# A decayed recurrence and two MoE layers on one core: the first 46 slots issued from a table of single operations, with six shared PSUM banks

## The chip, the core and the metric

The kernel runs on one core of a Trainium2 chip. The core has a matrix engine (TensorE, PE in the rows, with its weight loads as PEld), VectorE (DVE), ScalarE (ACT), GpSimd (POOL) and SyncE (SP), whose queue issues the transfers here. Each engine executes its own queue in order, and the engines wait for each other by semaphores. Times are device microseconds of one execution; less is better.

## The reference

What is computed, cut to what matters: a recurrence over 768 steps (2 batches, 8 heads, state 48 x 48), its output as 1536 tokens of 384 columns, a first two-layer MoE on them, and a second MoE with eight experts, whose weights P come from gates that are normalised by rows and columns eight times.

```python
for t in range(S):                       # r, k, v, w: [2, 8, 768, 48]
    cur = np.einsum('bhd,bhe->bhde', u[None] * kt, vt)
    y[:, :, t] = np.einsum('bhd,bhde->bhe', rt, state + cur)
    state = wt[:, :, :, None] * state + np.einsum('bhd,bhe->bhde', kt, vt)
x = y.transpose(0, 2, 1, 3).reshape(1536, 384)
h = x @ w_in                             # float64 weights, 384 x 2048
x = np.maximum(0.01 * h, h) @ w_out      # 2048 x 384
for e in range(8):                       # second MoE
    out += P[:, e:e + 1] * (np.maximum(x @ w1[e], 0.0) @ w2[e])
```

## The kernel before

**Recurrence.** The 1536 tokens are twelve tiles of 128 steps (`NBLK`), the two batches in turn. A tile is worked in chunk form by `att_steps` (L318): w, k and r are transposed on TensorE (four transposes each); VectorE makes the decays by two scans along time (L351, L355) and weighs K and R with them (L358, L361); TensorE forms scores (L382) and transposes K (L394); VectorE masks the scores (L400, two operations); TensorE forms the outputs from them and from the decayed state (L415, L426) and the next state (L435); VectorE adds (L446, L459); TensorE transposes y (L469), and ScalarE and VectorE write it as a rounded high part and a low part (L262, L263), which are the input of the first MoE.

**Weights of the first MoE.** They come as float64. A piece of 768 columns is loaded as words (L225) and put together by integer operations: four on VectorE (L231, L232, L235, L242), three on ScalarE, two on GpSimd (L247, L253). There are 16 such pieces, two staging buffers and two temporaries.

**Units of the first MoE.** A unit is one quarter of the hidden layer for 256 tokens; there are 24, in the list `order`. Each has two p1 slots (18 matmuls of 256 columns each, L497, into a bank `hb`, then relu parts: ScalarE L1003, VectorE L1004, ScalarE L1011, GpSimd L1012) and three p2 slots (12 matmuls each, L512, into `ybm`, then a sum into `x2f` on ScalarE L1023 or VectorE L1025). The p2 slots of a unit stand behind the p1 slots of the next one.

**What sets the order.** `slots` lists all p1 and p2 slots. The steps of the tiles and the pieces are attached to slots by number, in `ATT_AT`, `STEP_AT` and `PIECE_AT` (L778 to L780); slots below 0 come before the first unit. This written order is only what the framework's planner starts from: it moves instructions on each engine by its own estimate of times. Only the later part of the kernel, the second MoE, stands in a block `tc.manual_schedule()` (L1229), in which each engine keeps the written order. PSUM has eight banks: two for `ybm` and others (`py`), three for `hb` (`ph`), three for the recurrence (`pa`).

The rows name lines of this kernel. The tiles' loads come from L313 on SP's queue, two tiles ahead; the first of them, the vector u (L718) and the first two pieces are issued at the start.

Of the kernel before, what the change touches and what calls it, by code (L numbers as in the profile page):

```python
# [65 lines left out]
""".split()  # L66

# [13 lines left out]
def tile_rwkv__leaky_moe__sinkhorn_moe(  # L81
# [19 lines left out]
    P = 128  # L101
# [76 lines left out]
    def forward(general, ctx):  # L178
        def bank(which="a", name="bk"):
            pool = {"a": pa, "h": ph, "y": py}[which]  # L180
            t = pool.tile([P, 512], F32, tag="b" + which, name=name)
            return t
# [45 lines left out]
        def words_first(sv, nn):  # L228
            hw, lw = sv[:, :, :, 1], sv[:, :, :, 0]
            nv = nn.rearrange("p (a n) -> p a n", a=sv.shape[1])  # L230
            nc.vector.tensor_scalar(nv, hw, 11, -(2 ** 31), op0=ALU.logical_shift_left, op1=ALU.bitwise_or)  # L231
            nc.vector.scalar_tensor_tensor(  # L232
                out=nv, in0=lw, scalar=21, in1=nv, op0=ALU.logical_shift_right, op1=ALU.bitwise_or
            )
            nc.vector.tensor_scalar(lw, hw, 20, 0x7FF, op0=ALU.logical_shift_right, op1=ALU.bitwise_and)  # L235
            nc.scalar.activation(lw, lw, AF.Relu, scale=float(2 ** 23), bias=ebias[:, 0:1])

        def words_second(sv, nn, hi, lo, apart, lo_eng):
# [19 lines left out]
        def put_x(i, xb):  # L258
# [3 lines left out]
            nc.scalar.activation(xh, xv, AF.Copy)  # L262
            nc.vector.tensor_tensor(xl, xv, xh.bitcast(F32), op=ALU.subtract)  # L263
# [54 lines left out]
        def att_steps(i):  # L318
# [7 lines left out]
            def s0_pe():  # L326
                calls = []
                for n in ("w", "k", "r"):
                    st[n] = bank("a", f"t{n}")
                    for p in range(NP):  # L330
                        def f(n=n, p=p):
                            nc.tensor.transpose(
                                st[n][:, p * T : (p + 1) * T],
                                nat[n][:, 2 * p : 2 * p + 2, :].rearrange("p a d -> p (a d)"),
                                ident,
                            )
                        calls.append(f)
                return calls

            def s0_post():  # L340
# [5 lines left out]
                nc.gpsimd.tensor_tensor(A.rk, nat["r"][:, :, 0:D], nat["k"][:, :, 0:D], op=ALU.mult)  # L346
                nc.gpsimd.tensor_tensor(A.rk, A.rk, ub, op=ALU.mult)

            def s1_post():
                n = NP * LQ  # L350
# [3 lines left out]
                nc.vector.reciprocal(seg(A.rP, 0, 1), seg(A.q, 0, 1))  # L354
                nc.vector.tensor_tensor_scan(A.pf, A.wS[:, 0:n], A.rP, 1.0, op0=ALU.mult, op1=ALU.add)  # L355

            def s2_post():
                nc.vector.tensor_tensor(  # L358
                    A.K, st["k"].rearrange("p (a l) -> p a l", a=NP), seg(A.q, 1, T), op=ALU.mult
                )  # L360
                nc.vector.tensor_tensor(  # L361
                    A.R, st["r"].rearrange("p (a l) -> p a l", a=NP), seg(A.pf, 0, T), op=ALU.mult
                )
                for p in range(0 if first else NP):
# [4 lines left out]
                nc.scalar.activation(A.sq, A.q, AF.Square, accum_out=stat[:, 0, i : i + 1])  # L369
                nc.scalar.activation(A.sq, A.pf, AF.Square, accum_out=stat[:, 1, i : i + 1])  # L370
                nc.vector.tensor_reduce(out=A.cc, in_=A.rk, axis=AX.X, op=ALU.add)
                nc.gpsimd.tensor_tensor(
                    A.cv, nat["v"], A.cc.rearrange("p (h o) -> p h o", o=1).to_broadcast([P, H, D]), op=ALU.mult
                )

            def s3_pe():
                calls = []
                st["sc"] = [bank("a", f"sc{s}") for s in range(2)]
# [926 lines left out]
```

## Time and profile before

| | us |
|---|---|
| median of 3 runs (1115.46 to 1115.91) | 1115.6 |
| the profiled execution, whole | 1118.14 |
| its span, first to last instruction | 1116.3 |
| TensorE busy | 1078.4 (97%) |
| VectorE busy | 818.9 (73%) |
| GpSimd busy | 545.7 (49%) |
| ScalarE busy | 485.2 (43%) |
| mean granted TensorE clock | 0.978 |

The span is the profiled execution without what lies before its first and after its last instruction. Matmuls are pipelined: one that takes 0.28 us in a row may start 0.12 us behind the one before it, so the time of a run of matmuls is read from where the next one starts. The granted clock of TensorE is given as a share of full speed; before 37 us the rows show 1.00, but the matmuls take as long as at half speed.

### The profile page before, as it was taken

What the parts mean: (1) busy time and instruction counts of PE and PEld (TensorE: products, weight loads), DVE (VectorE), ACT (ScalarE), POOL (GpSimd) and SP (SyncE); (2) the same over time, 40 slices, a digit from 0 to 9 for tenths busy, and PEclk for the clock granted to TensorE, in tenths of its full rate; (3) what the DMA queues carried; (4) which work ended last, traced back from release to release, by engine and by line L of the source; (5) the groups of instructions that cost most, each with busy time, mean ns of one, the idle gap of its engine ahead of it and who ended that gap; (6) DMA issues with size and microseconds to landing.
All of it is one profiled execution on the core that took longest, in us unless ns stands there. A gap on an engine that the chain in (4) does not pass through costs nothing.

```text
span 1116.3 us, 16388 instructions
## 1 busy us (share of the span) xinstructions
PE 1078.4 (97%) x6295; PEld 993.1 (89%) x6295; DVE 818.9 (73%) x1352; ACT 485.2 (43%) x894; POOL 545.7 (49%) x632
## 2 busy tenths in 40 slices
PE   6898999998999799999999999999999999999997
PEld 5787999998998688899999999999999999999997
DVE  7889855457336889877777677777778777787775
ACT  4555534444334433374444444444444444435431
POOL 6767632257633444455544555445544455445510
PEclk9877999999999999999999999999999999999999
DMA  8444431003000010001100010000100001000002
GB/s 198 107 124 110 118 67 23 1 8 121 30 1 1 29 29 29 29 29 50 37 29 29 29 58 29 29 29 29 57 30 29 29 31 56 29 29 29 15 2 88
DMA packets 79160, 50.90 MB, mean 46 GB/s; under 512 B 51808, under 2 KB 73952, under 8 KB 79072
## 3 DMA queue, kind: packets, MB, share of 16 engines
q1 hardware_dynamic: 79072, 49.76, 15.3%
q8 instruction: 51, 0.84, 0.3%
q14 instruction: 37, 0.30, 0.1%
HBM read 47.39 MB, written 2.36 MB: 45 GB/s over the span
## 4 chain that ended last, share of the span: by engine, by line
PE 87%; DVE 8%; POOL 1%; DMA 1%; SPq 1%; ACT 1%; issue 1%; DVEq 0%; ACTq 0%; POOLq 0%
PE yb L1158 35%; PE m L1115 29%; PE ybm L512 8%; PE hb L497 7%; PE yb L426 2%; PE sc L382 2%; DVE nn L232 1%; PE m L1126 1%; PE sb L435 1%; DVE stg L242 1%; PE yb L415 1%; SPq L313 1%; DVE q L351 1%; DVE m L915 1%; DVE stg L235 0%
## 5 line engine op out<-in xcount | busy, mean ns | idle before, releaser
L1158 PE MATMUL yb<-w,wb 128*128 128x384 f32 x1392 | 278.3, 338 | 3.8 <-DVE small L610 1.5
L1173 DVE SCALAR_TENSOR_TENSOR x2f<-yb,Pm,x2f 128x384 f32<-128x384 f32 x336 | 205.4, 612 | 94.1 <-PE yb L1158 92.6
L1158 PEld LDWEIGHTS yb<-w,wb 128*128 128x128 f32 x1392 | 248.8, 189 | 23.4 <-DVE small L610 1.9
L868 POOL TENSOR_TENSOR w<-stg,w 128x768 fp32r<-128x768 f32 x32 | 59.2, 1850 | 369.4 <-ACT w L866 369.4
L1115 PE MATMUL m<-xr,wc 128*128 128x512 f32 x837 | 231.5, 396 | 0.0
L1187 ACT ACTIVATE sn<-m 128x512 f32<-128x512 f32 x217 | 129.0, 595 | 147.7 <-PE m L1115 147.6
L1158 PE MATMUL yb<-w,hs 128*128 128x384 f32 x912 | 181.5, 337 | 0.6 <-DVE x2f L1173 0.5
L1115 PEld LDWEIGHTS m<-xr,wc 128*128 128x128 f32 x837 | 155.2, 188 | 23.6
L1158 PEld LDWEIGHTS yb<-w,hs 128*128 128x128 f32 x912 | 162.7, 188 | 12.7 <-DVE x2f L1171 1.0
L1195 ACT ACTIVATE wb<-m 128x512 fp32r<-128x512 f32 x79 | 47.0, 597 | 148.4 <-PE m L1115 148.4
L1012 POOL TENSOR_TENSOR gl<-t,gh 128x512 fp32r<-128x512 f32 x48 | 70.5, 1474 | 78.7 <-ACT gh L1011 59.2
L897 POOL TENSOR_TENSOR wc<-wsum,wc 128x768 fp32r<-128x768 f32 (+1 forms) x60 | 101.3, 1709 | 0.0
L512 PE MATMUL ybm<-gh,wb 128*128 128x256 f32 x576 | 89.3, 295 | 3.1 <-DVE x2f L1025 3.1
L915 DVE TENSOR_TENSOR m<-m,sn 128x512 f32<-128x512 f32 x124 | 86.1, 694 | 5.3 <-ACT sn L1187 0.3
L512 PEld LDWEIGHTS ybm<-gh,wb 128*128 128x128 f32 x576 | 78.7, 199 | 6.3 <-DVE x2f L1025 3.5
L879 POOL TENSOR_TENSOR wsum<-stg 128x128 f32<-128x128 f32 x186 | 83.3, 469 | 0.9 <-DVE wc L897 0.9
L917 DVE TENSOR_TENSOR m<-sn,m 128x512 f32<-128x512 f32 x93 | 64.7, 695 | 25.2 <-PE m L1115 25.1
L1115 PE MATMUL m<-wahi,wc 128*128 128x512 f32 x279 | 81.0, 398 | 0.5 <-DVE m L915 0.5
L1115 PE MATMUL m<-walo,wc 128*128 128x512 f32 x279 | 81.0, 398 | 0.4 <-DVE m L915 0.2
L1195 ACT ACTIVATE hs<-m 128x512 fp32r<-128x512 f32 x51 | 30.5, 598 | 107.9 <-PE m L1115 107.9
L497 PE MATMUL hb<-xr,wahi 128*128 128x256 f32 x432 | 71.5, 289 | 0.2 <-DVE t L1004 0.2
L1004 DVE SCALAR_TENSOR_TENSOR t<-hb,t 128x512 f32<-128x512 f32 x48 | 32.8, 685 | 43.9 <-ACT t L1003 43.9
(173 smaller groups left out, 1730.7 us busy)
## 6 DMA issues: line engine op xcount, KB each, us to landing
stg<-in_moe_w_dram SPq DMA_DIRECT2D x64, 384.0 KB, 3.5
stg<-in_moe_w_in_dram SPq DMA_DIRECT2D x8, 768.0 KB, 5.1
stg<-in_moe_w_out_dram SPq DMA_DIRECT2D x8, 768.0 KB, 4.6
wn<-in_w_dram SPq DMA_DIRECT2D x12, 192.0 KB, 3.2
rn<-in_r_dram SPq DMA_DIRECT2D x12, 192.0 KB, 3.6
kn<-in_k_dram SPq DMA_DIRECT2D x12, 192.0 KB, 3.6
vn<-in_v_dram SPq DMA_DIRECT2D x12, 192.0 KB, 2.8
out_dram<-x2f SPq DMA_DIRECT2D x12, 192.0 KB, 1.9
```

The costliest lines, as they stand in the source:

```text
L497: nc.tensor.matmul(hb[:, s * GC : (s + 1) * GC], wt[:, c, f0 : f0 + P], x_part(xt, c, g * GC, GC), start=(n == 0), stop=(n == 3 * KD - 1),)
L512: nc.tensor.matmul(yb[:, :GC], wt[:, j, d * P : (d + 1) * P], gt[:, j, :], start=(n == 0), stop=(n == 3 * NJ - 1),)
L879: nc.gpsimd.tensor_tensor(sums[:, n, :], get(x), get(y), op=ALU.add if sg > 0 else ALU.subtract)
L897: eng.tensor_tensor(l, src, h.bitcast(F32), op=ALU.subtract)
L915: eng.tensor_tensor(out, x, y, op=ALU.add if sy > 0 else ALU.subtract)
L917: eng.tensor_tensor(out, y, x, op=ALU.subtract)
L1012: nc.gpsimd.tensor_tensor(gl[:, 2 * j : 2 * j + 2, :], tv, gv.bitcast(F32), op=ALU.subtract)
L1115: nc.tensor.matmul(b, wt, xt, start=start and k == 0, stop=k == 2, skip_group_check=True)
L1158: nc.tensor.matmul(yb[:, :DM], hv[:, hk, i, t * P : (t + 1) * P], wv[:, wk, i, :], start=n == 0, stop=n == 5)
L1173: nc.vector.scalar_tensor_tensor(out=av, in0=yb, scalar=Pm[:, i, e : e + 1], in1=av, op0=ALU.mult, op1=ALU.add)
L1187: nc.scalar.activation(t, psum(S, f[1]), AF.Copy)
L1195: nc.scalar.activation(h, v, AF.Relu)
```

## The change

The recurrence, pieces 0 to 8 and slots 0 to 45 are issued from a table, `FRONT`, inside `tc.manual_schedule()`, so each engine keeps the table's order. A word of the table is one operation or one group of matmuls. `5q` is an operation of tile 5, by a letter of `att_ops`: w k r the transposes, W the copy of w (ScalarE), q and p the two scans, I the reciprocal, K and R the weighing, a b v the bonus term (GpSimd), c its sum (VectorE), S s t ScalarE's work on the state and the range flags, m the scores, B and C the transpose of K and its copy, A and D the two masks, y the outputs, z the state, Y and U their sums, x the transpose of y, h and l its two parts. `5Lw` loads w of tile 5. `c3a` is an operation of piece 3: a b d f on VectorE, e g h on ScalarE, m l on GpSimd, L the load. `u2.1P` is the first matmul group of unit 2, half 1 (18 matmuls); r t h l are its relu parts on ScalarE, VectorE, ScalarE and GpSimd; `u2.1p` is its second group for output part 1 (12 matmuls), and q its sum into `x2f`.

In the front six banks are taken and given back in turn by the recurrence and by the first matmul groups, in place of three and three; two remain for the second groups. After the front, three banks are opened for the remaining p1 slots. The loads of the tiles stand in the table. Pieces 9 to 15 stay attached to slots; the loads of pieces 9 and 10 are written behind the front. The functions of steps are cut into single operations with the same instructions (`words`, `att_ops`, `m1_act`, `m1_sum`); a general path for other inputs, which is not run here, gets its bank from another pool.

```diff
+FRONT = """
+0w 0a 0k 0W 0r 0q 0b 1w 0s 0I 0K 0p 0B 0c 0C c0a 0t 0R 1r 1W c0b 0m 0v 1q c0g c0d 1a 1s 1k 0A 0z c0e 0D 1b 1I 1K
+0y 0U c0f 1p c0m 1B 2Lw 1C 0Y 2Lk 1t 1z 1c 1R c0h 1v 2Lr c1a c0l 2Lv 0x 1U c1b 1m 0h c2L 2a 0l 2w c1g 1A 2k 2W
+2r 1D 2b 2q 1y c1d 2s 2I 2K 3Lw c1e 1Y 2B 3Lk 2p 2S 1x 3Lr 2c 2C 3w 2R 3Lv 1h 2v 2t c1f 2m 3W 1l 3a 3k 3q 2z c1m
+3r 2A u0.0P 3s 2D 2U 3b c1h c3L 3I 3K 2y u0.0r 3p c1l u0.0t 3t 3c u0.0h c2a 3B 3S 4Lw 2Y u0.0l u0.1P 3R 4Lk 3C
+c2b 3v 4Lr c3a 2x c2g 4Lv 3m c2d u0.1r c3b 2h 4w c2e 4k 4a u0.1t 2l 4W 3z 3A u0.1h 4b 4r 3D c3g 4q 3y u0.1l 3U
+4s 4I c2f 4K c2m 4S 5Lw 3Y 4B 4p 5Lk 3x 4C 5Lr c2h 4z 4c 5Lv 3h c2l 4R 4t c4L 3l 4m c3d 5w 4v 4A 5k c3e 5r 4D 5a
+u2.0P 5W c3f 5b 5q 4y u2.0r c3m u2.0t 5s 4U 5I 5K c3h c5L u2.1P 5p 5S c3l 4Y 5t 5c 4x 5R 5B 5v 4h c4a u0.0p 5C
+6Lw 4l 6Lk c4b 5m u0.0q 6Lr c5a c4g 5z c4d 6Lv 5A c4e 6w 5D 6k 6W u0.1p 5U 6a 6q 5y u0.1q 6b c4f 6s 6I 6K c4m 6r
+6p 6S 7Lw 6B u0.2p 7Lk 6C c4h 5Y 7Lr 6z 6c u0.2q c4l u2.0h 6R 7Lv 5x 6t 6U 7w c6L 6m 5h c5b 7W u2.0l 7k 5l c5g
+7r 6A u1.0P 6D 6v 7q 7a 6y c5d u1.0r 7b 7s u1.0t c5e 7I 7K 7p u1.0h 7B 7S 8Lw u1.0l u3.0P 6Y 8Lk 7c 7t 7R 7v 8Lr
+u2.1r c5f 7C 6x 8Lv 7m 6h u2.1t c5m 6l 8w u2.1h 8k 7A 8W 7z 7D u2.1l c5h c7L 8q 8r 7y 8a 7U 8s 8I 8K c5l 8p
+u2.0p 8S 9Lw 9Lk 8B u2.0q 8b u1.1P 7Y 8C 9Lr 8R 8t 8c 9Lv c7a 8v c6a 7x u1.1r 8m 9a 7h u1.1t 9w 7l u1.1h 9k 8A
+9b 9W 8z 8D 9q 9r u1.1l 8y 8U 9s 9I 9K u3.0r 9p 9B 9S 10Lw u2.1p u3.0t 8Y 10Lk 9t 9c 8x 10Lr 9R 9C 9v u2.2p
+u2.1q c7b 8h 10Lv 9m 8l c7g c7d 10a c6b u2.2q 10w c7e 10k 9z 10W 10b 9A c6g 10r 9D u3.1P 10q 9U 10s 10I 9y 10K
+u3.1r 10p u3.1t 10t 10c u4.0P 10S 11Lw 9Y 10R 10v 11Lk c7f 11Lr 9x u4.0r c6d 10m c7m 9h 11Lv u4.0t c6e 9l 11w
+11k 10A u4.0h u4.1P 11a 11W 10D c7h c6f u4.0l 11q 10y 11b 11s 11I 11K c7l 11p 11r 11S u5.0P c6m 10Y 11t 11c 10x
+11R u5.1P 10h 11v c6h c8L 10l c6l 11m u5.1r u5.1t u6.0P 11A 11D 11y c8a c8b c8g c8d u1.0p 11Y c8e c8f 11x u1.1p
+11h u1.0q c8m 11l u1.2p u1.1q c8h u6.1P u1.2q u3.0h c8l u3.1h u7.0P u3.0l u7.1P u3.1l u4.1r u4.1t u4.1h u5.0r
+u3.0p u4.1l u5.0t u3.1p u3.0q u6.0r u6.0t u3.2p u3.1q u4.0p u5.0h u3.2q u5.1h u5.0l u4.1p u4.0q u5.1l u6.1r
+u4.2p u4.1q u6.1t u7.0r u5.0p u4.2q u7.0t u6.0h u6.1h u6.0l u5.1p u5.0q u6.1l u7.1r u5.2p u5.1q u7.1t u8.0P
+u5.2q u7.0h u7.1h u7.0l u6.0p u8.0r u7.1l u8.0t u6.1p u6.0q u6.2p u6.1q u7.0p u8.0h u6.2q u8.0l u7.1p u7.0q
+u7.2p u7.1q u8.1P u7.2q u9.0P u8.1r u8.1t u8.1h u9.1P u8.1l u9.0r u9.0t u9.0h u8.0p u9.0l u9.1r u9.1t u8.1p
+u9.1h u8.0q u9.1l u8.1q
+""".split()
+
+FRONT_SLOTS, FRONT_PIECES = 46, 9
...
-            pool = {"a": pa, "h": ph, "y": py}[which]
+            pool = {"h": ph[-1], "y": py}[which]
...
-        ph_cm = tc.tile_pool(name="ph", bufs=3, space=PSUM)
-        ph = ph_cm.__enter__()
-        pa_cm = tc.tile_pool(name="pa", bufs=3, space=PSUM)
-        pa = pa_cm.__enter__()
+        ph_cm = tc.tile_pool(name="pa", bufs=3, space=PSUM)
+        ph = [ph_cm.__enter__()]
+        if not general:
+            ph_cm.__exit__(None, None, None)
...
-        for i in range(0 if general else NBLK):
-            for n, stp in enumerate(att_steps(i)):
-                attach(ATT_AT[i] + STEP_AT[n], *stp, first=n < 2)
-            if i + 2 < NBLK:
-                attach(ATT_AT[i] + STEP_AT[4], none, lambda i=i: load_tile(i + 2, "wkrv"))
...
-            attach(at, none, lambda n=n: piece_a(n))
-            attach(at + 1, none, lambda n=n: piece_b(n))
+            if general or n >= FRONT_PIECES:
+                attach(at, none, lambda n=n: piece_a(n))
+                attach(at + 1, none, lambda n=n: piece_b(n))
...
-        close_slot = ATT_AT[-1] + STEP_AT[-1] + 2
+        close_slot = FRONT_SLOTS
...
+        def front():
+
+            pool_cm = tc.tile_pool(name="pf", bufs=1, space=PSUM)
+            pool = pool_cm.__enter__()
+            free = []
+            for n in range(6):
+                t = pool.tile([P, 512], F32, name=f"f{n}")
+                free.append(t)
+
+            def take():
+                return free.pop(0)
+
+            give = free.append
+            att = [att_ops(i, take, give) for i in range(NBLK)]
+            conv = {}
+            un = {}
+            for token in FRONT:
+                if token[0] == "c":
+                    n, x = int(token[1:-1]), token[-1]
+                    if x == "L":
+                        piece_load(n)
+                        continue
+                    if n not in conv:
+                        conv[n] = piece_ops(n)
+                    conv[n][x]()
+                elif token[0] == "u":
+                    n, j = (int(x) for x in token[1:-1].split("."))
+                    x = token[-1]
+                    q, g = order[n]
+                    gh, gl = gbuf[n % 2]
+                    if x == "P":
+                        un[n, j] = take(), tmps[(2 * n + j) % NTMP]
+                        for f in m1_p1(q, g, j, win(q), un[n, j][0])[1]:
+                            f()
+                    elif x in "rthl":
+                        m1_act(x, *un[n, j], gh, gl, j)
+                        if x == "t":
+                            give(un[n, j][0])
+                    elif x == "p":
+                        yb = bank("y", "ybm")
+                        un[n, j, "y"] = yb
+                        for f in m1_p2(q, j, yb, gh, gl, wout):
+                            f()
+                    else:
+                        m1_sum(un.pop((n, j, "y")), j, q, g)
+                elif "L" in token:
+                    i, x = token.split("L")
+                    load_tile(int(i), x)
+                else:
+                    att[int(token[:-1])][token[-1]]()
+            pool_cm.__exit__(None, None, None)
...
-        for sl in range(min(extra), 0):
-            run(sl, [], lambda: None)
+        if general:
+            for sl in range(min(extra), 0):
+                run(sl, [], lambda: None)
+        else:
+            with tc.manual_schedule():
+                front()
+            for n in range(2):
+                piece_load(FRONT_PIECES + n)
+        ph_cm = tc.tile_pool(name="ph", bufs=3, space=PSUM)
+        ph.append(ph_cm.__enter__())
         tcount = 0
         for sl, (kind, n, j) in enumerate(slots):
             q, g = order[n]
             gh, gl = gbuf[n % 2]
+            if not general and sl < FRONT_SLOTS:
+                tcount += kind == "p1"
+                continue
```

## Rows read from the trace of the kernel before

**Rows 1.** page, part 2: granted TensorE clock in 40 equal slices of the span, in tenths

```profile
PEclk9877999999999999999999999999999999999999
```

**Rows 2.** windows: stretch, length, busy us of each engine (instructions), granted clock, DMA share, GB/s

```profile
0.00:5.40 5.40, 1.09 (x4) 0.72 (x4) 1.66 (x10) 1.87 (x2) 2.71 (x16) 1.00 0.69 137
5.40:130.00 124.60, 108.55 (x676) 101.73 (x677) 108.47 (x137) 64.44 (x126) 89.54 (x54) 0.84 0.53 134
40.00:130.00 90.00, 79.67 (x528) 74.80 (x527) 79.87 (x101) 49.61 (x98) 67.31 (x39) 0.77 0.46 118
130.00:214.00 84.00, 83.74 (x745) 82.37 (x743) 49.53 (x82) 36.11 (x86) 27.86 (x23) 1.00 0.19 41
0.00:214.00 214.00, 193.37 (x1422) 184.82 (x1423) 159.65 (x228) 102.42 (x213) 120.11 (x93) 0.90 0.40 98
```

**Rows 3.** windows, same columns: a stretch in which TensorE waits

```profile
54.00:58.00 4.00, 0.26 (x1) 0.26 (x2) 4.00 (x5) 1.67 (x3) 2.60 (x1) 0.51 0.11 15
```

**Rows 4.** windows of L512 and of L497 alone; chain of waits: start, us, what

```profile
0.00:214.00 214.00, 47.85 (x298) 42.48 (x299) 0.90 0.40 98
...
0.00:214.00 214.00, 51.47 (x360) 45.86 (x360) 0.90 0.40 98
...
213.88 2.04 PE ybm L512 x17
...
221.92 2.88 PE ybm L512 x24
```

**Rows 5.** timeline of TensorE, tiles at full clock: start, us, engine, line, what

```profile
154.81 1.16 PE L382 MATMUL sc<-R,K 48*128 48x128 f32 x16 [0.26 <-DVE R L361]
...
155.90 0.62 PE L497 MATMUL hb<-xr,wahi 128*128 128x256 f32 x3
...
160.73 0.36 PE L415 MATMUL yb<-Sp,R 128*128 128x96 f32 x2
...
163.34 1.10 PE L435 MATMUL sb<-vn,Kb 128*128 128x96 f32 x8
...
164.28 0.60 PE L332 MATMUL tw<-ident,wn 128*128 128x128 f32 x4
...
164.63 0.61 PE L497 MATMUL hb<-xr,wahi 128*128 128x256 f32 x3
```

**Rows 6.** groups of VectorE up to 214 us: line, names, count, busy us, mean ns, idle

```profile
L232 DVE SCALAR_TENSOR_TENSOR nn<-stg,nn 128x768 int32<-128x768 int32 x12 | 16.6, 1385 | 0.3
...
L242 DVE SCALAR_TENSOR_TENSOR stg<-stg 128x768 int32<-128x768 int32 x12 | 15.5, 1290 | 3.4 <-ACT stg L236 3.4
...
L1004 DVE SCALAR_TENSOR_TENSOR t<-hb,t 128x512 f32<-128x512 f32 x20 | 13.5, 681 | 10.7 <-ACT t L1003 10.7
...
L235 DVE TENSOR_SCALAR stg<-stg 128x768 int32<-128x768 int32 x12 | 11.1, 926 | 0.1
...
L231 DVE TENSOR_SCALAR nn<-stg 128x768 int32<-128x768 int32 x12 | 10.2, 849 | 1.6 <-DMA stg<-in_moe_w_in_dram 1.5
...
L446 DVE TENSOR_TENSOR y<-yb,cv 128x384 f32<-128x384 f32 x12 | 6.6, 550 | 15.7 <-PE yb L426 15.7
...
L1025 DVE TENSOR_TENSOR x2f<-ybm,x2f 128x256 f32<-128x256 f32 x12 | 5.0, 420 | 2.2 <-PE ybm L512 2.1
...
L527 DVE TENSOR_TENSOR wgp<-wg,wgp 128x24 fp32r<-128x24 f32 x1 | 1.6, 1607 | 0.0
```

**Rows 7.** timeline of the start, VectorE and GpSimd: idle before and its end in brackets

```profile
9.06 0.67 DVE L361 TENSOR_TENSOR R<-tr,pf 128x512 f32<-128x512 f32 x1
...
10.59 1.77 POOL L347 TENSOR_TENSOR rk<-rk,spare 128x384 f32<-128x384 f32 x1 [3.12 <-DMA spare<-in_u_dram]
```

**Rows 8.** timeline of TensorE where its clock came up

```profile
36.25 0.96 PE L497 MATMUL hb<-xr,wahi 128*128 128x256 f32 x3
...
37.05 0.52 PE L497 MATMUL hb<-xr,walo 128*128 128x256 f32 x3
```

**Rows 9.** windows, columns as in the second group: behind the old front

```profile
214.00:238.00 24.00, 24.00 (x202) 24.00 (x202) 4.73 (x9) 9.55 (x19) 7.62 (x6) 1.00 0.01 1
```

More of the change, by code (lines that the diff above doesn't have):

```diff
@@ L316, in seg, with att_ops @@
             return t[:, 0 : NP * LQ].rearrange("p (a l) -> p a l", a=NP)[:, :, lo : lo + n]
-        def att_steps(i):
+        def att_ops(i, take, give):
             nat = A.nat[i % 2]
@@ L368, in s2_post, with scores @@
                     )
[L369 to L378, printed above, removed]
+            def scores():
+                put("s0")
+                put("s1")
@@ L390, in s3_pe @@
-                if not last:
-                    st["kb"] = bank("a", "kb")
-                    for p in range(NP):
-                        def f(p=p):
-                            nc.tensor.transpose(st["kb"][:, p * T : (p + 1) * T], A.K[:, p, :], ident)
-                        calls.append(f)
-                return calls
-            def s3_post():
-                for s in range(2):
+                        nc.tensor.matmul(
+                            st[f"s{s}"][:, p * T : (p + 1) * T],
+                            A.K[s * 64 : s * 64 + D, p, :],
+                            A.R[s * 64 : s * 64 + D, p, :],
+                            start=True,
+                            stop=True,
+                        )
@@ L405, in s3_post, with copy_k, outputs @@
                     )
-                if not last:
-                    nc.scalar.activation(A.Kb, st["kb"].rearrange("p (a t) -> p a t", a=NP), AF.Copy)
-            def s5_pe():
-                calls = []
-                st["y"] = bank("a", "yb")
+                    give(st[f"s{s}"])
+                return f
+            def copy_k():
+                nc.scalar.activation(A.Kb, st["kb"].rearrange("p (a t) -> p a t", a=NP), AF.Copy)
+                give(st["kb"])
+            def outputs():
+                put("y")
@@ L446, in s5_post, with states, add_y @@
+            def states():
+                put("s")
+                for p in range(NP):
+                    nc.tensor.matmul(
+                        st["s"][:, 2 * p * D : 2 * (p + 1) * D],
+                        A.Kb[:, p, :],
+                        nat["v"][:, 2 * p : 2 * p + 2, :].rearrange("p s d -> p (s d)"),
+                        start=True,
+                        stop=True,
+                    )
+            def add_y():
                 nc.vector.tensor_tensor(
@@ L463, in s7_pe, with add_s @@
-            def s7_pe():
-                st["x"] = bank("a", "xb")
+                give(st["y"])
+            def add_s():
+                pv = st["s"][:, : H * D].rearrange("p (a s d) -> p a s d", a=NP, s=2)
+                for s in range(2):
+                    rows = slice(s * 64, s * 64 + 64)
+                    if first:
+                        nc.scalar.activation(A.S[b][rows, :, s, :], pv[rows, :, s, :], AF.Copy)
+                    else:
+                        nc.vector.tensor_tensor(
+                            A.S[b][rows, :, s, :], pv[rows, :, s, :], A.Sp[rows, :, s, :], op=ALU.add
+                        )
+                give(st["s"])
@@ L489, in m1_p1 @@
+        def m1_p1(q, g, j, win, hb=None):
+            if hb is None:
+                hb = bank("h", "hb1")
             calls = []
```

269 lines of the change are left out of this document (130 added, 139 removed).

## The prediction

> **What bounds the kernel now.** I read the page's 40 slices first, for TensorE's granted clock: only the first eight slices, some 130 us, and one short dip later fall below full speed [rows 1]. Then the windows, which give each engine's busy time by stretch. From 130 to 214 us TensorE is busy 83.74 of 84 us at full clock: nothing but less TensorE work would shorten that. From 40 to 130 us it is busy 79.67 of 90 us, but at a mean clock of 0.77, while VectorE is busy 79.87 us [rows 2]. Two things cost time there. VectorE orders the recurrence and is idle 124.6 - 108.5 = 16.1 us between 5.4 and 130 us [rows 2]. And TensorE, waiting for it, drops to the lower of its two levels (1.2 GHz): in a stretch where it has 0.26 us of work in 4 us and VectorE works all the time, the clock is 0.51 [rows 3]. A mean of 0.77 over 90 us is (1 - 0.77) x 90 x 2 = 41 us at the lower level, a loss of 20.7 us, beside 10.3 us of idle time.
>
> **Where the old front ends.** The change rewrites slots 0 to 45: twelve tiles, pieces 0 to 8, both halves of the first matmul of units 0 to 9, and the second matmul of units 0 to 7 and two thirds of unit 8. That is 10 x 36 = 360 matmuls of L497 and 8 x 36 + 24 = 312 of L512. By 214 us there are 360 and 298; the run of 17 that starts at 213.88 holds the 312th and ends at 215.9 us [rows 4]. The recurrence is over by then too. From there TensorE is full, so what the front wins or loses moves the end by as much. The question is when the new front ends, called T below; the old T is 215.9.
>
> **TensorE's work in the front.** At full clock 24 matmuls take 2.88 us, 0.12 each [rows 4]: 672 x 0.12 = 80.6 us. For the recurrence I take start-to-start times [rows 5]: scores 155.90 - 154.81 = 1.09 us; outputs 163.34 - 160.73 = 2.61; states 0.94; four transposes 0.35. Twelve tiles: 46 groups of four transposes (w, k, r, and ten of K) 16.1, scores 13.1, outputs 31.3 less 2 for the first two tiles, which lack the decayed state, states 9.4 (ten tiles), three transposes of y 12 x 0.26 = 3.1; together 71. In all 151.6 us.
>
> The table fixes TensorE's order, so its tail can be counted. After `11y`, the last outputs, there are 366 matmuls (`u1.0p` to `u8.1p`) and `11x`: 43.9 + 0.3 = **44.2 us**. Nothing long stands in that tail's way: its VectorE work is 17 us (below). So T = end of `11y` + 44.2, and `11y` is reached either by VectorE or by TensorE, whichever is later.
>
> **Path by VectorE.** Up to 214 us VectorE was busy 159.65 us [rows 2]. From that I take what the new front does not hold: 1.66 us before 5.4 us [rows 2]; 1.6 for the gate weights' low part (moved behind the front) [rows 6]; three of the twelve pieces already converted by 214 us, each 0.85 + 1.39 + 0.93 + 1.29 = 4.45, so 13.4 [rows 6]; and I add 0.55 for the twelfth low part. Left: 143.6 us. Behind `11D` stand piece 8 (4.45), `11Y` and `11l` (1.1), ten `t` of units (6.8) and twelve `q` (5.0): 17.4 [rows 6]. So 126.2 us must run before `11D` ends, from 5.4 us on.
>
> To that come stalls S. Nothing in the trace of before shows the new order's stalls, so I bound them: 0 below, and above by twice the old rate. One of them is visible. The table puts `0c` ahead of `0R` on VectorE, and `0c` needs `0b` on GpSimd, which waited for `u` from memory until 10.59 us and took 1.77 [rows 7]. In the old order `R` went first, at 9.06, ahead of that wait. So VectorE will stand from about 9.2 to 12.4, with the scores of tile 0 behind it: some 3 us. I take S at the old rate, 16.1 / 108.5 = 15%, because many other joins are covered: between `5R` and `5A` stand four piece operations and `4l`, over 3 us, against the 1.09 of the scores; the thinnest is `4R`, `3l`, `c3d`, `4A`. S = 18.7. End of `11D` = 5.4 + 126.2 + 18.7 = 150.3; with outputs 2.6 and the tail 44.2, **T = 197.1**. With S = 6, T = 184; with S = 37, T = 216.
>
> **Path by TensorE.** Its clock came up at about 37 us in the old front: three matmuls took 0.96 us at 36.25 and 0.52 at 37.05 [rows 8]. By then it had done tiles 0 and 1 and two groups of transposes, 11.8 us of full-clock work; walking the first tokens of the table with the stall above, the new order is at the same place at 37. To the end of `11y` remain 151.6 - 44.2 - 11.8 = 95.6 us, where the old order needed 151.6 - 85.9 - 11.8 = 53.9 between 37 and 130. So TensorE has far more to do in this stretch, and its clock matters more. With the old idle time (10.3) and no drop of the clock: 37 + 95.6 + 10.3 = 142.9, earlier than VectorE's path, which then decides (197.1). With the old 41 us at the lower level as well: 142.9 + 20.7 = 163.6, **T = 207.8**. [...] I take the middle of the two, **T = 202.5**, a gain of 13.4 us.
>
> **Edits costed at nothing.** ScalarE and GpSimd execute the same operations; ScalarE is busy 102.4 and GpSimd 120.1 of 214 us [rows 2]. The tiles' loads move on SP's queue from fixed places to places in the table, each still a tile ahead; if a load came late by 1 us, VectorE's `q` of that tile would wait as long. Six shared banks in place of three and three remove bank waits, which I take at nothing. After the front three banks are opened anew; slot 46 (12 matmuls, 1.44 us) covers the release by the last `r` and `t`, one `t` of 0.68 us [rows 6] and an operation like it before it; without that cover it costs 1.4 us. Pieces 9 to 11 were converted inside the old front and now come behind it. Their 13.4 us of VectorE work lies where VectorE is busy only 4.73 of 24 us [rows 9], and piece 9 is due 12 slots, some 21 us, after slot 46. I take 0; without that cover it is up to 13.4 us, a rival below.
>
> **The rivals.**
> (1) *Hardly any stalls*: S near 6 and the clock up. T = 184 to 192; 24 to 32 us less, 1084 to 1092. For it: VectorE's joins are covered. Against it: the first 37 us win nothing, and both paths are tight at once.
> (2) *The clock*: TensorE does not get its 95.6 us through. It decides from the point where idle time plus half the time at the lower level exceeds 215.9 - 44.2 - 37 - 95.6 = 39.1 us; the old front had 31.0 of this in its 90 us. If their shares stay as they were (11.5% idle, 46% at the lower level), each microsecond does 0.655: 95.6 / 0.655 = 146, T = 37 + 146 + 44.2 = 227, so 11 us slower, about 1127. For it: the dips after waits [rows 3]. Against it: a longer queue of ready matmuls.
> The Trainium skill ("TensorE: Matmul & The Clock Gate", section "A second HAM failure mode: psum-queue depth-cycling") says that a kernel cycling through PSUM banks can idle so often and so briefly between groups of matmuls that its clock swings between the two levels. Six banks handed round are such a cycle; by this rule the share of 46% would stay or grow, and rival (2) would be the result. The trace agrees only in part: the dips before follow long waits, not short ones.
> (3) *Given back*: pieces 9 to 11 delay slots 57 to 66 by most of 13.4 us; about 1115, no change. Against it: VectorE's idle time there.
> (4) A front that does not follow its table can be left aside: it is issued in written order.
>
> **How the numbers follow.** The profiled execution has a span of 1116.3 and took 1118.1; the median is 1115.6, so differences are taken from the span and put on the median. Forecast: 1115.6 - 13.4 = **1102.2**, own range 1094 to 1112 (T from 194 to 212), chance 0.57. Rival (1) 0.15, rival (2) 0.16, rival (3) 0.12. The range that should hold 8 in 10 reaches into both sides: **1088 to 1119**. Faster or slower by 0.2% (2.2 us) is about what can be told from no change. Faster: 0.57 + 0.15 = 0.72; same 0.11; slower 0.17, mostly rival (2).
>
> **What would show it.** In the profile after: the 312th matmul of the second kind near 202 us; `11y` ending near 158; VectorE idle 15 to 22 us before the last mask; granted clock at the lower level for 10 to 30 us between 37 and 158; a wait of VectorE or GpSimd for `u` near 10 us; TensorE solid afterwards. Wrong if the clock stays low through whole tiles, if VectorE stands for TensorE at each tile's scores (S above 37), or if TensorE waits in slots 57 to 66.

## The result, and the profile after

The changed kernel takes 1106.85 us, the median of four runs (1104.46 to 1107.35), against 1115.53 of the kernel before, timed beside it: a ratio of 0.9915, with a 95% interval of 0.9902 to 0.9928. That is 8.7 us less by the medians, and 0.85% by the ratio. Forecast were 1102.2, with 1088 to 1119.

The profiled execution after took 1104.46 us, with a span of 1102.7, and is the shortest of its four. So its profile shows 13.6 us less span than before, 5 more than the medians differ; where that comes from is told below.

First the granted clock in 40 slices, to be laid beside [rows 1]: the first three slices are low now, and the sixth, in place of the second to the fourth.

```profile
PEclk8889989999999999999999999999999999999999
```

Then the end of the front. In the chain of waits (start, us, what) the 24 matmuls of L546, the old L512, that complete the 312 stand at 201.27, and the first slot behind the table follows without a gap:

```profile
194.79 6.48 PE f L531 x54
201.27 2.88 PE ybm L546 x24
204.15 2.16 PE hb L531 x18
```

The front ends at 204.15, where the old one ended at 215.9 [rows 4]: 11.7 of the 13.6 us. The windows tell what TensorE made of the time (stretch, its length, busy us of PE, PEld, DVE, ACT and POOL with instructions, granted clock, DMA share, GB/s). After:

```profile
0.00:37.00 37.00, 28.06 (x186) 25.25 (x187) 29.71 (x52) 17.70 (x39) 23.01 (x30) 0.91 0.65 155
37.00:130.00 93.00, 86.44 (x713) 81.94 (x713) 86.83 (x121) 53.63 (x119) 53.49 (x38) 0.91 0.48 111
...
130.00:160.00 30.00, 25.54 (x192) 24.52 (x191) 21.49 (x30) 13.20 (x23) 19.36 (x12) 0.84 0.26 80
...
160.00:204.00 44.00, 43.00 (x352) 42.46 (x352) 19.20 (x30) 19.66 (x35) 23.59 (x17) 0.99 0.18 55
```

and the same stretches of before, as far as they differ:

```profile
0.00:37.00 37.00, 26.97 (x129) 24.65 (x130) 27.29 (x45) 15.00 (x28) 23.24 (x30) 1.00 0.67 158
...
37.00:130.00 93.00, 82.67 (x553) 77.80 (x552) 82.83 (x103) 51.32 (x100) 69.01 (x41) 0.78 0.48 124
130.00:160.00 30.00, 29.74 (x265) 29.13 (x263) 19.68 (x33) 13.99 (x33) 11.85 (x9) 1.00 0.37 80
```

Between 37 and 130 us TensorE is idle 6.6 us in place of 10.3, and the mean clock is 0.91 in place of 0.78, worth (0.91 - 0.78) x 93 = 12.1 us: 15.9 us won, three quarters of it through the clock. Before 37 us TensorE does 57 more instructions; in the profiles of e9 and e10 below, which keep nearly the same table, it is 35 and 32, so part of the 57 belongs to this execution. Between 130 and 160 it loses again: 4.5 us idle in place of 0.3, and 0.16 x 30 = 4.8 us of clock. Here the loss has one place. VectorE (timeline: start, us, engine, line, operation, out<-in, the idle time before it and who ended it):

```profile
140.94 0.56 DVE L299 TENSOR_TENSOR xr<-f,xr 128x384 fp32r<-128x384 f32 x1
147.61 0.56 DVE L264 TENSOR_SCALAR nn<-stg 128x768 int32<-128x768 int32 x1 [6.12 <-DMA stg<-in_moe_w_in_dram]
148.21 0.96 DVE L267 SCALAR_TENSOR_TENSOR nn<-stg,nn 128x768 int32<-128x768 int32 x1
149.08 0.68 DVE L1083 SCALAR_TENSOR_TENSOR t<-f,t 128x512 f32<-128x512 f32 x1
149.68 0.55 DVE L270 TENSOR_SCALAR stg<-stg 128x768 int32<-128x768 int32 x1
150.15 1.28 DVE L429 TENSOR_TENSOR AT<-f,spare 128x512 f32<-128x512 f32 x2
```

The operation at 147.61 is the first of weight piece 9. That piece is no part of the table; it is attached to slots behind it. The planner, which orders whatever stands outside the manual block, put it into VectorE's queue between the table's `10l` and `u5.1t`, and its weights landed only at 147.5. Their load had waited for a staging buffer, which GpSimd gave back at 142.8, and takes 4.7 us. Behind it stood `u5.1t`, which gives back the bank that `11y` needs, and then the last masks, `11A` and `11D`. TensorE in the same stretch:

```profile
145.45 0.52 PE L531 MATMUL f<-xr,wahi 128*128 128x256 f32 x3
149.82 0.46 PE L446 MATMUL f<-Sp,R 128*128 128x96 f32 x2 [3.85 <-DVE t L1083]
150.89 1.25 PE L455 MATMUL f<-vn,AT 128*128 128x48 f32 x4 [0.60 <-DVE AT L429]
...
155.00 0.98 PE L455 MATMUL f<-vn,AT 128*128 128x48 f32 x4
155.77 2.06 PE L546 MATMUL ybm<-gh,wb 128*128 128x256 f32 x8
```

It waits 3.85 us, and then `11y` takes 5.9 us, against 2.6 at full clock [rows 5]. A second wait of this kind stands at 45 to 49 us: `3z` needs the bank of `u0.1t`, and four operations of pieces 2 and 3 stand ahead of that on VectorE.

```profile
49.05 2.02 PE L463 MATMUL f<-vn,Kb 128*128 128x96 f32 x8 [3.43 <-DVE t L1083]
```

```profile
43.30 1.02 DVE L267 SCALAR_TENSOR_TENSOR nn<-stg,nn 128x768 int32<-128x768 int32 x1
44.25 1.20 DVE L264 TENSOR_SCALAR nn<-stg 128x768 int32<-128x768 int32 x1
45.36 1.36 DVE L270 TENSOR_SCALAR stg<-stg 128x768 int32<-128x768 int32 x1
46.64 1.75 DVE L267 SCALAR_TENSOR_TENSOR nn<-stg,nn 128x768 int32<-128x768 int32 x1
48.32 0.68 DVE L1083 SCALAR_TENSOR_TENSOR t<-f,t 128x512 f32<-128x512 f32 x1
```

The granted clock is 0.50 from 48 to 62 us. Both waits are for a bank of the shared six; in the kernel before no matmul of the front waited for a unit's `t` longer than 0.2 us. At `11y` the bank is only what was missing first: the outputs need the masks too, and `11A` starts at 150.15, behind the same wait for piece 9.

### The profile page after: what moved, and what is told of

Read it like the earlier page. It is cut to its first block, busy times and chain, and to the rows that moved or that the text cites. A ratio compares the mean times of both kernels' runs of the same rounds, so it can differ in the third digit from the quotient of the medians.

```text
span 1102.7 us, 16354 instructions
## 1 busy us (share of the span) xinstructions
PE 1066.0 (97%) x6295; PEld 980.7 (89%) x6295; DVE 815.4 (74%) x1352; ACT 485.9 (44%) x894; POOL 544.6 (49%) x632
## 4 chain that ended last, share of the span: by engine, by line
PE 81%; DVE 12%; POOL 3%; issue 1%; DMA 1%; ACT 1%; SPq 0%; POOLq 0%; DVEq 0%; ACTq 0%
PE yb L1266 35%; PE m L1223 29%; PE ybm L546 7%; PE hb L531 5%; DVE pf L392 1%; DVE nn L264 1%; DVE nn L267 1%; DVE q L387 1%; PE f L531 1%; PE m L1234 1%; DVE AT L429 1%; DVE t L1083 1%; POOL nn L278 1%; PE f L463 1%; DVE stg L274 1%
## 5 line engine op out<-in xcount | busy, mean ns | idle before, releaser
L1087 POOL TENSOR_TENSOR gl<-t,gh 128x512 fp32r<-128x512 f32 x48 | 67.3, 1406 | 70.5 <-ACT gh L1085 48.1
L546 PE MATMUL ybm<-gh,wb 128*128 128x256 f32 x576 | 84.0, 289 | 3.0 <-DVE x2f L1094 3.0
L546 PEld LDWEIGHTS ybm<-gh,wb 128*128 128x128 f32 x576 | 75.9, 195 | 4.8 <-DVE x2f L1094 3.3
L1305 DVE SCALAR_TENSOR_TENSOR wb<-m,wb 128x512 fp32r<-128x512 f32 x79 | 54.3, 687 | 10.6 <-ACT wb L1303 8.7
L1223 PEld LDWEIGHTS m<-wahi,wc 128*128 128x128 f32 x279 | 51.2, 188 | 7.5 <-DVE m L950 0.8
```

Of the source, the lines that this page charges most:

```text
L546: nc.tensor.matmul(yb[:, :GC], wt[:, j, d * P : (d + 1) * P], gt[:, j, :], start=(n == 0), stop=(n == 3 * NJ - 1),)
L1087: nc.gpsimd.tensor_tensor(gl[:, 2 * j : 2 * j + 2, :], tv, gv.bitcast(F32), op=ALU.subtract)
L1223: nc.tensor.matmul(b, wt, xt, start=start and k == 0, stop=k == 2, skip_group_check=True)
```

## The experiments

The times are medians of four runs. The kernel before, timed beside each, lay between 1114.75 and 1115.70. "Slot 46" is the start of the first matmul of the first slot behind the table (the planner put one with 18 matmuls first), from the timeline of the profiled execution. These times hold for one execution each, and two of them, those of the changed kernel and of e4, had TensorE's clock up early, as told below. The theory: VectorE's path sets the front's end, the fixed order keeps it nearly full, and what is still lost lies in the two waits for banks. The rivals: TensorE or the units' chain sets it anyway, so that a wait taken away comes back elsewhere; or the banks, not the order, bring the gain.

| kernel | us | ratio to before, 95% | slot 46 at |
|---|---|---|---|
| changed kernel | 1106.85 | 0.9915 (0.9902 to 0.9928) | 203.99 |
| e1 six banks, old order | 1131.18 | 1.0146 (1.0129 to 1.0163) | |
| e2 table, planner free | 1127.73 | 1.0114 (1.0097 to 1.0130) | |
| e3 pieces 9, 10 held | 1101.72 | 0.9873 (0.9857 to 0.9890) | 201.16 |
| e4 `u0.1t` earlier | 1103.81 | 0.9897 (0.9881 to 0.9914) | 202.85 |
| e5 both, `0c` behind `0R` | 1098.64 | 0.9854 (0.9838 to 0.9871) | 197.65 |
| e6 = e5, masks twice | 1103.39 | 0.9893 (0.9876 to 0.9909) | 201.96 |
| e7 = e5, `Kb` copies thrice | 1098.95 | 0.9852 (0.9836 to 0.9869) | 199.09 |
| e8 = e5, pieces spread | 1098.90 | 0.9845 (0.9828 to 0.9862) | 198.12 |
| e9 `0c` behind `0R` alone | 1106.01 | 0.9903 (0.9882 to 0.9924) | 206.46 |
| e10 scores of group 11 four times | 1107.16 | 0.9921 (0.9904 to 0.9937) | 207.56 |
| e11 = e5, `c3a`, `c3b` later | 1099.09 | 0.9863 (0.9846 to 0.9879) | 197.37 |
| e12 = e5, conversion left out | 1094.15 | 0.9814 (0.9784 to 0.9845) | 194.97 |

**The parts of the change, each alone.** e1 gives the kernel before the shared banks:

```diff
-            t = pool.tile([P, 512], F32, tag="b" + which, name=name)
+            t = pool.tile([P, 512], F32, tag="by" if which == "y" else "bs", name=name)
...
-        ph_cm = tc.tile_pool(name="ph", bufs=3, space=PSUM)
-        ph = ph_cm.__enter__()
-        pa_cm = tc.tile_pool(name="pa", bufs=3, space=PSUM)
-        pa = pa_cm.__enter__()
+        ph_cm = tc.tile_pool(name="ph", bufs=6, space=PSUM)
+        ph = pa = ph_cm.__enter__()
```

> The kernel before with its six PSUM banks as one pool for the recurrence and the first-MoE units, in the order that the planner makes; no table. Theory A (the table's order brings the gain, and the shared banks only make that order possible): within 2.2 us of the kernel before, 1113 to 1117 us. Theory B (waits for a bank are what the old front lost): 1111 us or less. Theory C (the shared pool lets units take banks that the recurrence then waits for): 1118 us or more.

It is 15.5 us slower than before, the side of theory C, though not by its mechanism. The waits of TensorE up to 205 us (operation <- releaser: us in total, times, longest):

```profile
PE sc L380 <- DVE R L359: 16.5, 3, 7.2
PE xb L467 <- DVE y L444: 13.4, 5, 7.4
```

These are not waits for a bank, but for VectorE's results: offered other banks, the planner made another order, in which VectorE starts 13 piece operations between 36.5 and 63 us, against 10 before. Six banks alone bring nothing here.

e2 keeps the table as the written order and takes the block away that holds the planner to it:

```diff
-            with tc.manual_schedule():
-                front()
+            front()
```

> The changed kernel with its table as the written order alone: the planner is free to move the table's operations. Theory A (it is the fixed order of the front that brings the gain): the end of the front falls back towards that of before, the 312th L546 matmul at 210 us or later, the whole 1111 to 1117 us. Theory B (writing the operations one by one in this order is enough, the planner keeps near to it): 1104 to 1109 us.

It is 20.9 us slower than the changed kernel and 12.5 slower than before, worse than theory A had it. Its stretch from 37 to 130 us:

```profile
37.00:130.00 93.00, 78.06 (x474) 73.28 (x474) 86.99 (x104) 50.74 (x96) 66.32 (x39) 0.79 0.49 124
```

VectorE is as busy as in the changed kernel, but with fewer operations, and TensorE gets 474 instructions through in place of 713. Of the 239 that are missing, 77 belong to units and 162 to the recurrence itself, whose last outputs start 30 us later. The outputs in e2, then in the changed kernel (ns, first and last start):

```profile
L455 PE MATMUL f<-vn,AT x192: 203/275/449, 15.1 to 185.9; 128*128 128x48 f32 x192
L455 PE MATMUL f<-vn,AT x192: 234/275/448, 17.3 to 155.6; 128*128 128x48 f32 x192
```

What VectorE did instead are the weight pieces: 38 of their operations in this stretch, 49.6 us, against 22 and 25.9 us in the changed kernel and 36 and 42.3 us in the kernel before. One of the four kinds, in this order:

```profile
L267 DVE SCALAR_TENSOR_TENSOR nn<-stg,nn 128x768 int32<-128x768 int32 x9 | 15.0, 1667 | 0.1
L267 DVE SCALAR_TENSOR_TENSOR nn<-stg,nn 128x768 int32<-128x768 int32 x6 | 8.4, 1404 | 0.0
L232 DVE SCALAR_TENSOR_TENSOR nn<-stg,nn 128x768 int32<-128x768 int32 x9 | 13.8, 1529 | 0.2
```

So it is the fixed order that brings the gain, and neither the list as such nor the banks alone; much of what it does is to hold the pieces back on VectorE. Two rivals were not run: the table with three and three banks, and the planner's order with the pieces attached to later slots.

**The wait for piece 9.** e3 makes piece 9 and most of piece 10 members of the table's tail; their loads move into the table with them.

```diff
-FRONT_SLOTS, FRONT_PIECES = 46, 9
+FRONT_SLOTS, FRONT_PIECES = 46, 11
...
-... u4.1p u4.0q u5.1l u6.1r u4.2p u4.1q u6.1t u7.0r u5.0p u4.2q u7.0t u6.0h ...
+... u4.1p u4.0q u5.1l c9a c9b u6.1r u4.2p u4.1q u6.1t u7.0r u5.0p u4.2q u7.0t c9g c9d c9e c9f u6.0h ...
```

> Weight piece 9 and most of piece 10 are made members of the table's tail, behind the operations of the front they now overtake; nothing is left out. Theory A (what the front still loses is the 6.1 us that VectorE waits for piece 9's weights with u5.1t and 11A queued behind it, the 2.1 us of that piece's two operations there, and the lower clock that follows): 11D ends near 143 us, 11y near 147, the 312th L546 matmul at 192 to 197 us in place of 204.2, the whole 1095 to 1101 us. Theory B (the wait only covers another one: TensorE's own remaining work or the units' activations decide when the slots begin, or the slots 57 to 66 then wait for the later pieces and give it back): within 2 us of the changed kernel, 1105 to 1109 us.

It is 5.1 us less, between the theories: 0.7 us above theory A's range, 3.3 below B's. VectorE's timeline where the wait was, and TensorE's, which has neither the wait nor the lower clock:

```profile
146.71 0.69 DVE L1087 SCALAR_TENSOR_TENSOR t<-f,t 128x512 f32<-128x512 f32 x1 [2.70 <-ACT t L1085]
147.32 1.28 DVE L430 TENSOR_TENSOR AT<-f,spare 128x512 f32<-128x512 f32 x2
```

```profile
148.32 0.36 PE L447 MATMUL f<-Sp,R 128*128 128x96 f32 x2
148.52 0.57 PE L456 MATMUL f<-vn,AT 128*128 128x48 f32 x4
...
150.53 0.57 PE L456 MATMUL f<-vn,AT 128*128 128x48 f32 x4
150.92 1.20 PE L547 MATMUL ybm<-gh,wb 128*128 128x256 f32 x8
```

`11y` takes 2.6 us. The rest of the expected gain is given back: between 160 and 205 us TensorE is busy 41.25 of 45 us, against 44.00 in the changed kernel. The pieces' work now lies there; how much of these waits is theirs, e8 and e12 ask.

**The wait of `3z`.** e4 moves two operations of one unit:

```diff
-4Lk 3C c2b 3v 4Lr c3a 2x c2g 4Lv 3m c2d u0.1r c3b 2h 4w c2e 4k 4a u0.1t 2l
+4Lk 3C u0.1r c2b u0.1t 3v 4Lr c3a 2x c2g 4Lv 3m c2d c3b 2h 4w c2e 4k 4a 2l
```

> Only u0.1r (ScalarE) and u0.1t (VectorE) stand earlier in the table, u0.1t ahead of four piece operations, so that its bank comes back to 3z earlier. Theory A (the shared banks made this wait, and the clock of the next 12 us follows from it): the wait of 3.4 us ahead of 3z falls under 1 us, the granted clock from 48 to 62 us stays above 0.8, and the whole is 2 to 6 us below the changed kernel, 1101 to 1105 us. Theory B (VectorE's own work between 70 and 140 us sets 11D, so an earlier TensorE is only earlier at waiting): the wait goes, 11D still ends at 150 to 152 us, and the whole stays within 1.5 us of the changed kernel.

Theory A: 3.0 us less. The two intervals overlap a little, but all four runs lie below all four of the changed kernel, and the same edit on top of e3 brings 3.1 us again (e5). The wait of 3.4 us is gone from the list, though three smaller ones for `K` add up to 4.5 us, and the mean clock from 48 to 62 us is 0.76 in place of 0.50, a little under the 0.8 expected.

**Together.** e5 is e3 and e4, and moves `0c` behind `0R`:

```diff
-0p 0B 0c 0C c0a 0t 0R 1r 1W
+0p 0B 0C c0a 0t 0R 0c 1r 1W
```

> The two edits of the other kernels together (pieces 9 and 10 held in the tail; u0.1r and u0.1t earlier), and 0c moved behind 0R, so that VectorE does not stand before the load of u at 8 to 10.6 us. Theory A (three separate losses on VectorE's path): 11D near 139 to 142 us, the 312th L546 matmul near 189 to 193, the whole 1091 to 1097 us. Theory B (they cover each other, or TensorE's work is next late): 1099 us or more.

1098.64 us, 8.2 less than the changed kernel, where e3 and e4 add up to 8.2: two separate losses. `0c` has nothing left to itself, and e9, which moves it alone, says the same:

> The changed kernel with 0c alone moved behind 0R, so that VectorE works on R while the load of u and GpSimd's product with it are under way. Theory A (the 2.5 us wait ahead of 0c is on the path that ends the front): the wait falls under 1 us and the whole is 1 to 2.5 us below the changed kernel. Theory B (the first groups are held by the loads of their inputs, or the later waits for piece 9 and for u0.1t take up what is won): within 0.8 us of the changed kernel.

0.8 us less by the medians, with intervals that overlap: no gain that can be told. Theory B.

**Whose path it is.** e6 issues ten masks twice; e7 issues copies on ScalarE three times, in the same groups. They are eight copies more and not ten, since tile 10 has none, so 8 x 0.60 = 4.8 us in place of the 5.9 of its expectation:

```diff
-                    nc.vector.tensor_tensor(
+                    for _ in range(2 if 6 <= i <= 10 else 1):
+                        nc.vector.tensor_tensor(
```

```diff
-                nc.scalar.activation(A.Kb, st["kb"].rearrange("p (a t) -> p a t", a=NP), AF.Copy)
+                for _ in range(3 if 6 <= i <= 10 else 1):
+                    nc.scalar.activation(A.Kb, st["kb"].rearrange("p (a t) -> p a t", a=NP), AF.Copy)
```

> The kernel with pieces 9 and 10 held, u0.1r and u0.1t earlier and 0c behind 0R (1098.6 us), with both mask multiplications of groups 6 to 10 issued twice, which leaves the output as it was: ten more VectorE operations of 0.68 us, 6.8 us of work, between 75 and 140 us. Theory A (VectorE's path sets the end of the front): 11D and the whole 5 to 7 us later, 1103.5 to 1106 us. Theory B (TensorE's own work sets it, VectorE is busy only because it is ahead): at most 2 us more, 1098 to 1100.7 us.

> The same kernel of 1098.6 us, with the Kb copy of groups 6 to 10 issued three times in place of once on ScalarE: ten more operations of 0.59 us, 5.9 us of ScalarE work in the same stretch. Theory A (VectorE's path decides, ScalarE has slack there, 17.9 us busy of 30): at most 1.5 us more, 1098 to 1100.2 us. Theory B (any engine's delay in a fixed order comes through to the end): 4 to 6 us more, 1102.5 to 1104.7 us.

6.8 us more on VectorE cost 4.75 us, just under theory A's range and far from B's; 4.8 us more on ScalarE cost 0.3. The last masks of e5, e6 and e7 (min/median/max ns, first and last start from 130 us on), in this order:

```profile
L430 DVE TENSOR_TENSOR AT<-f,spare x4: 677/679/680, 131.7 to 144.4; 128x512 f32<-128x512 f32 x4
```

```profile
L431 DVE TENSOR_TENSOR AT<-f,spare x6: 675/682/692, 135.7 to 149.2; 128x512 f32<-128x512 f32 x6
```

```profile
L430 DVE TENSOR_TENSOR AT<-f,spare x4: 675/678/681, 134.6 to 147.3; 128x512 f32<-128x512 f32 x4
```

`11D` comes 4.8 us later by VectorE's load and 2.9 by ScalarE's; of the latter 1.4 us are left at slot 46, and as much in the whole of that execution, the longest of e7's four. So VectorE's path is the one that counts, not all of it (some 70% of an added microsecond), and ScalarE's slack is real but short. No run that told adds work to TensorE here, which in the changed kernel is busy 67.1 us between 70 and 140; how close behind its own path lies is not shown.

**What the late pieces cost.** e8 moves the operations of pieces 9 and 10 into earlier gaps of the tail; e12 leaves their conversion out.

```diff
-u1.2p u1.1q c8h ... u1.2q u3.0h ... u5.1l c9a c9b u6.1r ... u7.0t c9g c9d c9e c9f ... u8.0t c10a c10b
+... u1.2q c9a c9b c9g u3.0h ... u4.1t c9d c9e ... u5.0t c9f c9m ... u5.1l c10a c10b c9l ... u7.0t c10g c10d c10e
```

> The same kernel of 1098.6 us, with the operations of pieces 9 and 10 moved forward in the table's tail, from 163 to 195 us into VectorE's gaps between 152 and 170 us. Theory A (the 3.7 us for which TensorE still waits between 160 and 205 us come from the late pieces' operations standing ahead of the units' t and sums): 2 to 4 us less, 1094.5 to 1096.6 us. Theory B (those waits belong to the units' own chain of r, t, h, l, so that the pieces only fill them): within 1 us, 1097.6 to 1099.6 us.

> The kernel of 1098.6 us (pieces held, u0.1r and u0.1t earlier, 0c behind 0R) without the operations a, b, d, e, f, g and m of weight pieces 9 and 10, which are left out of the computation: their loads and their last two operations stay. It prices what the two pieces cost in the tail, where TensorE still waits 3.7 us between 160 and 205 us. Theory A (those waits come from the pieces' operations on VectorE, ScalarE and GpSimd, which have to be done somewhere): the first matmul of the first slot behind the table stands 2.5 to 4 us earlier than at 197.65 us, and the whole is 2 to 4 us less, 1094.6 to 1096.6 us. Theory B (they belong to the units' own chain of r, t, h and l): within 1 us, 1097.6 to 1099.6 us.

e8 changes nothing (+0.3 us): in place of a wait of 1.9 us that ends at 179.6, TensorE now waits 2.7 us until 165.2, for a unit's sum on VectorE, ahead of which a unit's `t` stands that came late from ScalarE, and a piece operation. e12 takes 4.5 us less by the medians (its four runs spread from 1091.7 to 1097.7, and its interval overlaps that of e5), and slot 46 comes 2.7 us earlier; but TensorE is still idle 2.85 us between 160 and 205 us, and 2.75 of them are one wait for a unit's sum, until 164.3. So pieces 9 and 10 cost some 4 us by the medians, known only roughly since the spread is wide, and part of TensorE's waits there belongs to the units' own chain. Which part of e12's gain lies behind slot 46 was not followed up.

**Two that did not tell.** e10 fills TensorE's wait ahead of `11y` with repeated scores, to price the clock drop by itself:

```diff
-                for p in range(NP):
+                for p in [p for _ in range(4 if i == NBLK - 1 else 1) for p in range(NP)]:
```

> The changed kernel with the 16 score matmuls of group 11 (11m) issued four times in place of once, which leaves the output as it was: 3.5 us of extra TensorE work between 143 and 147 us, ahead of the 3.9 us for which TensorE waits there, so that this wait shrinks to about 0.4 us while 11A still begins near 150 us. Theory A (the wait's clock drop is a loss of its own, 5.9 us for the 11y that take 2.6 at the full clock): the granted clock from 145 to 160 us stays above 0.9 in place of 0.68, 11y ends near 152.5 in place of 155.8, and the first matmul of the first slot behind the table stands 2 to 3.5 us earlier than at 204.2. Theory B (the drop is hidden, or the extra work is paid for in full): that matmul stands within 1 us of 204.2, or up to 3.5 us later.

The time is that of the changed kernel (+0.3 us), but the planner put one more operation of piece 9 (its fourth, L274) ahead of `11A`, and TensorE then waited in the middle of `11y`:

```profile
152.79 0.46 PE L446 MATMUL f<-Sp,R 128*128 128x96 f32 x2 [1.31 <-DVE t L1083]
155.85 0.42 PE L455 MATMUL f<-vn,AT 128*128 128x48 f32 x2 [2.60 <-DVE AT L429]
```

The clock fell all the same, only later (0.66 from 156 to 166 us). The price of the drop by itself stays open. e11 moves `c3a` and `c3b` behind `3D`:

```diff
-u0.1r c2b u0.1t 3v 4Lr c3a 2x c2g 4Lv 3m c2d c3b 2h 4w c2e 4k 4a 2l 4W 3z 3A u0.1h 4b 4r 3D c3g
+u0.1r c2b u0.1t 3v 4Lr 2x c2g 4Lv 3m c2d 2h 4w c2e 4k 4a 2l 4W 3z 3A u0.1h 4b 4r 3D c3a c3b c3g
```

> The kernel of 1098.6 us (pieces held, u0.1r and u0.1t earlier, 0c behind 0R) with c3a and c3b moved behind 3D, so that 2l, which gives back the bank that the transposes of r in group 4 wait 2.4 us for at 49 us, stands 1.5 us earlier on VectorE. Theory A (bank waits here are set by which VectorE operations stand ahead of the one that gives back): that wait falls under 1.2 us and the whole is 0.5 to 2.5 us less. Theory B (VectorE is full until 145 us, so that any wait of TensorE before is paid for by VectorE's work anyway): within 0.8 us of 1098.6 us.

+0.45 us, theory B: the wait for `2l`'s bank goes, and a wait of 3.5 us for `K` takes its place. This shift of two piece operations wins nothing.

## Why the forecast held, step by step

**The front's end.** T was put at 202.5, and the profile has 204.15. That is near in part by luck. With the tail of 44.2 us the forecast had `11y` end at 158.3; it ended at 155.8, in an execution whose clock came up early. And the tail took 204.15 - 155.8 = 48.4: 1.0 us of idle time, and some microseconds at the lower clock after the wait. A front that ends earlier moves the end by as much: 11.7 of 13.6 us.

**VectorE's path.** 126.2 us of work and 18.7 of stalls after 5.4 us were to end `11D` at 150.3; it ended at 151.4, after 129.86 us of work and 16.2 of stalls. The size is right, the manner not. 2.1 us of the work are three operations of piece 9, which the forecast had behind the front. And between 70 and 140 us VectorE is busy 69.58 of 70 us, so the stalls are not spread over the joins, and 6.1 of them are the one wait for piece 9. e6 and e7 show that this path decides. Rows 1 were read too widely: no slice behind the fourth, which ends at 112 us, is below 90%; no term of the sum uses this.

**The visible stall.** `0c` before `0R` waits as forecast:

```profile
9.97 1.00 POOL L505 TENSOR_TENSOR rk<-rk,spare 128x384 f32<-128x384 f32 x1 [2.68 <-DMA spare<-in_u_dram]
...
11.00 0.55 DVE L510 TENSOR_REDUCE cc<-rk 128x8 f32<-128x384 f32 x1 [2.54 <-POOL rk L505]
```

But it is worth less than 1 us (e9): the matmuls behind it wait next for the loads of `w`, `r` and `k` (3.7, 2.3 and more us in e5).

**The clock.** From 37 to 158 us its mean is 0.90, that is 0.10 x 121 x 2 = 24 us at the lower level; 10 to 30 were forecast. Rival (2) did not come. The Trainium skill's section on depth-cycling ("TensorE: Matmul & The Clock Gate", "A second HAM failure mode: psum-queue depth-cycling") would have had six cycling banks swing the clock by many brief idle gaps; the trace disagrees: from 70 to 140 us, with the banks cycling and 2.9 us of idle time in short gaps, the clock is 1.00, and the two falls follow single waits of 3.4 and 3.9 us. But the forecast's reading of the kernel before, that its falls follow long waits and not short ones, holds for two of three only: that at about 99 us (0.50 from 100 to 112) came behind waits of 0.6, 0.6 and 1.5 us. What makes the clock fall behind some short waits and not behind others is not shown.

**Where it was too good.** 1102.2 was forecast and 1106.85 measured: 13.4 us of gain against 8.7. Three terms failed.
- Rival (4) was left aside with the sentence that the front "is issued in written order". Its own members are; but the planner puts others between them, and with piece 9 held the kernel takes 5.1 us less (e3).
- "Six shared banks [...] remove bank waits, which I take at nothing": there were two, of 3.4 and 3.9 us, because a bank comes back only when VectorE reaches a unit's `t`. The first cost 3.0 us (e4); the second is part of piece 9's, and the masks would have made most of it too. The three banks that are opened anew behind the front cost nothing in the changed kernel, though the 12 matmuls that were to cover them came only behind 18 others; in e5 TensorE waits 1.2 us there for the last `t`.
- Outputs of 2.6 us: `11y` took 5.9 at the lower clock. This too is in e3's 5.1 us.

The two together are 8.2 us, more than the miss; without them the kernel is 3.6 us below the forecast (e5).

**Pieces 9 to 11 at nothing.** Not so either: held in the tail, two of them cost some 4 us by the medians (e12), far from the 13.4 of rival (3). In the changed kernel this cost does not show in the slots, since it was paid within the front: VectorE is through with its work on twelve pieces by 205 us, as it was by 214 before [rows 6].

**Why the profile looks better than the median.** e10 has the same instructions as the changed kernel up to the scores of group 11, and these start at 145.28 us in its profile and at 142.46 in that of the changed kernel. In the latter the clock was up once already at 17 us (16 outputs in 1.93 us, against 3.54 in the profiles of e5 and e6 at the same place), which of the others only e4's shows (1.91 us). So some 3 us of the profile's 13.6 belong to this execution; by this estimate a common one ends its front near 207 us.

## What to carry to other kernels

A hand-written order fixes only the operations that are in it: look in the trace for what the planner has put between them, first on the engine whose queue decides, and take these neighbours (later weight pieces here) into the list. Where one pool of banks serves two chains, ask of each bank which operation gives it back and what stands ahead of that on its engine. And on a nearly full engine, shifting short operations (`0c`, `c3a` and `c3b`, the spread pieces) brought nothing three times over; the one shift that won, of `u0.1t`, gave back a bank that TensorE stood waiting for.

## What the runs showed of the hardware

VectorE's piece operations stretch beside GpSimd. `L270` took 0.55 us at 149.68 and 2.09 us at 153.67, while GpSimd's product of 2.49 us ran from 152.84 on:

```profile
152.84 2.49 POOL L278 TENSOR_TENSOR nn<-nn,stg 128x768 f32<-128x768 f32 x1 [7.24 <-DVE stg L274]
```

```profile
153.67 2.09 DVE L270 TENSOR_SCALAR stg<-stg 128x768 int32<-128x768 int32 x1
```

It ends 0.4 us after GpSimd does. The Trainium skill ("SBUF — State Buffer", "Who interferes with whom") says that such a VectorE instruction can take the port pair that it shares with GpSimd, and that whichever comes second stands until the other is done; the trace agrees. So the mean of 0.93 us for this operation in [rows 6] is no property of the operation, but of what runs beside it.

And the granted clock is no good witness in the first microseconds: the window from 0 to 37 us reads 1.00 before, though three matmuls at its end still take 0.96 us, against 0.52 right behind it [rows 8]; it reads 0.77 in e5 and 1.00 in e6, where most matmuls of that stretch have the same durations.
